# Last product of a long convolution in two column halves of TensorE, with the token rows of the input and the output stored even first, then odd

## The chip, the cores and the metric

The kernel runs on one core of a Trainium2 chip. The metric is the time of one execution on the device, in microseconds (us). Three runs of the kernel before gave 245.14, 244.03 and 245.14 us; their median is 245.14 us. The profile shows one more execution of the same program, with its own time.

The core has four compute engines that work beside each other: TensorE (PE in the profile, PEld for its weight loads), VectorE (DVE), ScalarE (ACT) and GpSimd (POOL). SyncE (SP) issues nearly all DMA transfers; a transfer, once issued, is carried out by some or all of 16 DMA engines.

## The reference

Two kinds of layer alternate, twice each, on x of 2048 tokens by 512 channels (bfloat16). Layer A is a gated long convolution, layer B an MLP of hidden width 1376. All weights are the same in both rounds.

```
def _A_ref(q, k, v, shift_k, ssm_k, ssm_D):
    ...
    k_shift = 4-tap causal convolution of k along the tokens, per channel
    kv = k_shift * v
    ...
    y = causal convolution of kv with ssm_k over 2048 tokens, by FFT
    y = y + kv * ssm_D[None, None, :]
    return q * y

def _B_ref(x, w1, b1, w2, b2):
    y = _layernorm(x, axis=-1)
    h = _gelu(jnp.einsum("bsd,df->bsf", y, w1) + b1)
    return jnp.einsum("bsf,fd->bsd", h, w2) + b2

x = A_q
x = x + _A_ref(_layernorm(x), A_k, A_v, A_shift_k, A_ssm_k, A_ssm_D)
x = x + _B_ref(_layernorm(x), B_w1, B_b1, B_w2, B_b2)
x = x + _A_ref(_layernorm(x), A_k, A_v, A_shift_k, A_ssm_k, A_ssm_D)
x = x + _B_ref(_layernorm(x), B_w1, B_b1, B_w2, B_b2)
```

(The shift and the convolution are given here in words.) Since k, v and the filters are the same in both rounds, the convolution result y is the same too, and the kernel computes it once.

## The kernel before

The kernel has two stages, and a pool of PSUM buffers for each.

**The convolution stage** (up to line 712) computes y by a transform of 2048 points that is split into factors of 32 and 64. Each factor is a matrix product with a table on TensorE; between the factors the data is turned by transposes, some on TensorE and some by DMA. Every step is a named piece, and the global order of all pieces, with the engine that runs each, is written out by hand in the string `ORDER`: `X32.P23` means that piece X32 runs on TensorE (P) and takes slot 2 of one ring of buffers and slot 3 of another; D, A, G and S are VectorE, ScalarE, GpSimd and the DMA queue of SyncE. Each engine executes its pieces strictly in that order, so a piece that has to wait holds everything that stands behind it on its engine. The pieces that matter here are:

- `lx0` (line 434) loads the first quarter of x, 4 tokens a partition, into `lna0` for the first LayerNorm. `lx` and `ly` (lines 499, 500) load x again into `x_t`, the first quarter and the other three. All three read the input `A_q` as `"(p nt) d -> p nt d"`: partition p holds the 16 tokens 16p to 16p+15, so one partition's share is one contiguous piece of memory. They are issued by SyncE through the helper `load` (line 280).
- `lk0`, `lk1`, `lv0`, `lv1` load k and v (line 280 too); `kT0` to `kT3` (line 423) transpose k on TensorE, `kT2` and `kT3` from `lk1`.
- `s00` (line 438) takes the LayerNorm statistics of `lna0` on VectorE.
- `U3T0` and `U3T1` (line 283) are DMA transposes of the first factor's result for the last quarter of the channels. `X30` and `X31` (line 515) read what U3T0 leaves, `X32` and `X33` what U3T1 leaves. In TensorE's order X32 comes before X31, and V10, X30 and the rest behind them.
- `Z01`, `Z00`, `Z20`, `Z21`, `Z03`, `Z23`, `Z10` and five more (line 584) are DMA transposes of the inverse transform's intermediate, in this order on the DMA queue behind lx; the first digit is the quarter of the channels, the second the group of tokens.
- `Y00`, `Y01`, `Y02`, `Y32`, `Y10`, `Y30`, `Y12`, `Y22`, `Y20` (line 610, in `last_mm`) are the last product. Each computes one or two columns of tokens: for every column the table `GPt`, 128 by 2 by 128, is multiplied with the two halves `V2[g][:, 0]` and `V2[g][:, 1]`, and the two products are added in PSUM. Of each 128-column half of the table, half of the columns are zero: half 0 of the table contributes to tokens of partitions with even p only, half 1 to those with odd p. Y00 needs Z00, Z10 and Z20.
- `g00` (line 635) multiplies the convolution result with the normalized x and adds it to x.

The helper `load` and its like issue a DMA whose access pattern on each side is a list of (step, count) pairs. The outermost pair comes first.

**The MLP loop** (lines 716 to 807) goes 8 times over groups of 512 tokens: `mm1` (line 726, evacuated by ScalarE with the GELU, line 728) and `mm2` (line 760, added to x by VectorE, line 765). In its second half each finished part of x is stored to the output by a DMA (line 767), 128 KB at a time, and at the very end twice 64 KB.

## Time and profile before

| | value |
|---|---|
| median of three runs | 245.14 us |
| time of the profiled execution | 245.1 us |
| its span in the profile | 243.1 us |
| convolution stage, until the MLP loop starts | 0 to 96.9 us |
| MLP loop | 96.9 to 239.5 us |
| last store, until the end | 239.5 to 243.1 us |

The span is the time between the first and the last instruction that the profiler recorded; the device time of the same execution is 2.0 us longer. In the profile, L610 is line 610 of the kernel, and "busy" of an engine counts its arithmetic alone. A row of the timeline merges successive instructions of one kind: start, length, engine, line, operation, count. SPq is SyncE's queue of DMA issues; its rows show how long the issue took, not the transfer. "us to landing" is the time from the start of an issue to the completion of the transfer.

### The profile page before, as it was taken

How to read it: one execution, taken by the hardware profiler on the slowest of the kernel's cores; microseconds unless marked ns; L12 is line 12 of the kernel's file. 1: busy time of each engine (PE TensorE's matmuls, PEld its weight loads, DVE VectorE, ACT ScalarE, POOL GpSimd, SP SyncE). 2: the span in 40 equal slices, each digit the busy share in tenths (PEclk: the TensorE clock that was granted, in tenths of full speed). 3: DMA queues.
4: the chain of work that ended last, by engine and by line, in shares of the span. 5: the costliest groups of instructions: out<-in, count | busy, mean ns of one | idle time of the engine just before them, and what ended most of it. 6: DMA issues, size and time to landing. Idle time of an engine off the chain costs nothing.

```text
span 243.1 us, 4771 instructions
## 1 busy us (share of the span) xinstructions
PE 230.3 (95%) x1941; PEld 138.5 (57%) x1941; DVE 168.2 (69%) x319; ACT 136.9 (56%) x193; POOL 38.4 (16%) x55
## 2 busy tenths in 40 slices
PE   6687999999997999999999999999999999999994
PEld 2675579889995598444444444444444444444443
DVE  0486988999998999698798977668757951031022
ACT  2563999899999998327117207307406505604700
POOL 5008694000000411301111011101101010000000
PEclk9999999999999999999999999999999999999999
DMA  8989979969899990403304030030033025011011
GB/s 133 193 235 392 380 270 379 386 146 270 197 163 171 317 250 12 86 0 25 65 0 88 0 71 18 0 74 13 4 91 83 0 62 113 0 43 43 3 43 43
DMA packets 56165, 29.55 MB, mean 122 GB/s; under 512 B 48618, under 2 KB 52431, under 8 KB 55248
## 3 DMA queue, kind: packets, MB, share of 16 engines
q1 hardware_dynamic: 56136, 29.25, 46.6%
q8 instruction: 15, 0.25, 0.4%
q14 instruction: 6, 0.05, 0.1%
q10 hardware_dynamic: 8, 0.00, 0.0%
HBM read 15.10 MB, written 2.10 MB: 71 GB/s over the span
## 4 chain that ended last, share of the span: by engine, by line
PE 80%; ACT 8%; SPq 6%; DMA 3%; issue 2%; DVE 0%; ACTq 0%
PE po L760 31%; PE ph L726 27%; PE p L670 4%; ACT ZT L212 4%; DMA Wt<-tabW 3%; SPq L280 3%; PE p L304 3%; SPq L343 3%; ACT arena L212 3%; PE p L610 3%; PE p L332 2%; PE p L538 2%; PE p L515 2%; ACT xb L212 2%; PE p L481 1%
## 5 line engine op out<-in xcount | busy, mean ns | idle before, releaser
L728 ACT ACTIVATE arena<-ph,B 128x512 bf16<-128x512 f32 (+1 forms) x77 | 52.9, 687 | 78.3 <-PE ph L726 78.2
L760 PE MATMUL po<-arena 128*128 128x512 bf16 (+2 forms) x363 | 77.4, 372 | 0.0
L726 PE MATMUL ph<-arena 128*128 128x512 bf16 (+1 forms) x308 | 67.6, 379 | 0.0
L760 PEld LDWEIGHTS <-arena 128*128 128x128 bf16 (+1 forms) x363 | 35.4, 98 | 40.5
L765 DVE TENSOR_TENSOR arena<-po,arena 128x512 bf16<-128x512 f32 (+1 forms) x33 | 21.6, 672 | 45.8 <-PE po L760 45.8
L726 PEld LDWEIGHTS <-arena 128*128 128x128 bf16 (+1 forms) x308 | 30.8, 100 | 35.9
L212 ACT ACTIVATE arena<-p 128x1024 bf16<-128x1024 f32 (+5 forms) x41 | 37.2, 1003 | 11.6 <-PE p L380 7.1
L250 POOL TENSOR_TENSOR lrsm<-lrsm,mhalf 128x4 f32<-128x4 f32 (+2 forms) x11 | 10.0, 911 | 96.9 <-DVE lrsm L244 96.9
L212 ACT ACTIVATE ZT<-p 128x1024 bf16<-128x1024 f32 (+1 forms) x26 | 24.7, 1050 | 0.9 <-PE p L304 0.8
L234 DVE BATCH_NORM_STATS2 lstm<-arena 128x6 f32<-128x512 bf16 x32 | 20.0, 681 | 0.2
L214 DVE CAST arena<-p 128x1024 bf16<-128x1024 f32 (+2 forms) x15 | 12.6, 905 | 11.0 <-PE p L374 9.7
L234 DVE BATCH_NORM_STATS2 lstg<-arena 128x6 f32<-128x512 bf16 x32 | 19.7, 678 | 0.0
L530 DVE TENSOR_TENSOR arena<-xb,arena 128x2048 bf16<-128x2048 bf16 (+1 forms) x17 | 18.9, 1153 | 0.8 <-ACT xb L212 0.7
L538 PE MATMUL p<-arena,arena 128*128 128x128 bf16 x256 | 16.1, 219 | 0.7 <-DVE arena L530 0.4
L538 PEld LDWEIGHTS <-arena 128*128 128x128 bf16 x256 | 14.8, 98 | 1.4 <-DVE arena L530 0.9
L250 POOL TENSOR_TENSOR lrsg<-lrsg,mhalf 128x4 f32<-128x4 f32 x8 | 8.1, 1012 | 41.5 <-DVE lrsg L247 41.5
L214 DVE COPY arena<-p 128x2048 bf16<-128x2048 bf16 (+2 forms) x12 | 13.3, 1109 | 1.8 <-PE p L423 1.6
L255 DVE TENSOR_SCALAR arena<-arena,lmvg,lrsg 128x512 bf16<-128x512 bf16 x28 | 9.7, 409 | 6.8 <-POOL lrsg L250 6.8
L212 ACT ACTIVATE xb<-p 128x1024 bf16<-128x1024 f32 x14 | 14.3, 1088 | 0.0
L255 DVE TENSOR_SCALAR arena<-arena,lmvm,lrsm 128x512 bf16<-128x512 bf16 x32 | 11.6, 416 | 2.4 <-POOL lrsm L250 2.4
L491 DVE TENSOR_TENSOR arena<-p,arena 128x1024 bf16<-128x1024 f32 x8 | 9.8, 1224 | 1.7 <-PE p L482 1.7
L678 ACT ACTIVATE arena<-p,B 128x128 bf16<-128x128 f32 (+3 forms) x33 | 10.0, 486 | 1.1 <-PE p L670 1.1
(70 smaller groups left out, 213.7 us busy)
## 6 DMA issues: line engine op xcount, KB each, us to landing
arena<-arena SPq DMA_DIRECT2D x8, 512.0 KB, 5.8
arena<-in_A_k_dram SPq DMA_DIRECT2D x2, 1024.0 KB, 9.7
arena<-in_A_v_dram SPq DMA_DIRECT2D x2, 1024.0 KB, 13.3
arena<-tabM SPq DMA_DIRECT2D x1, 2048.0 KB
out_dram<-arena SPq DMA_DIRECT2D x15, 128.0 KB, 1.7
arena<-in_A_ssm_k_dram SPq DMA_DIRECT2D x3, 512.0 KB, 5.6
arena<-in_A_q_dram SPq DMA_DIRECT2D x1, 1536.0 KB, 7.5
arena<-in_B_w_dram SPq DMA_DIRECT2D x1, 1376.0 KB, 6.4
```

The lines of the kernel that those rows point to most:

```text
L212: nc.scalar.activation(dst, src, AF.Copy)
L214: nc.vector.tensor_copy(dst, src)
L234: nc.vector.bn_stats(self.st[:, i, 0, :], x_t[:, GT * g + i, :] if src is None else src[:, i, :])
L250: nc.gpsimd.tensor_tensor(self.rs[:, a:b], self.rs[:, a:b], mhalf[:, a:b], ALU.pow)
L255: eng.tensor_scalar(out=dst[:, i, :], in0=xs, scalar1=self.mv[:, i, 0:1], scalar2=self.rs[:, i:i + 1], op0=ALU.subtract, op1=ALU.mult)
L530: eng.tensor_tensor(kk, x2, kk, ALU.mult)
L538: nc.tensor.matmul(o[:, i, :], spec[:, cc, ka + i, :], Mt[:, ka + i, r, :], start=r == 0, stop=r == 1)
L678: nc.scalar.activation(hT[0:m, ft, a * P:b * P], o[0:m, ft - f0, :], AF.Gelu_apprx_tanh, bias=B1[0:m, ft:ft + 1])
L726: nc.tensor.matmul(o.rearrange("p (i t) -> p i t", t=P), W1t[:, ct, ft * P:ft * P + m], lt[:, a:b, ct, :], start=ct == 0, stop=ct == CT - 1)
L728: nc.scalar.activation(hT[0:m, ft, a * P:b * P], o, AF.Gelu_apprx_tanh, bias=B1[0:m, ft:ft + 1])
L760: nc.tensor.matmul(po[:, a:b], hT[0:m, ft, i * P:(i + 1) * P], W2t[0:m, ft, a:b], start=ft == 0, stop=ft == FT - 1)
L765: nc.vector.tensor_tensor(xs, po[:, a:b], xs, ALU.add)
```

## The change

The table of the last product is cut to the columns that are not zero: half x keeps the columns of the partitions with p mod 2 = x, so `GPt` is 128 by 2 by 64. The two products of a column are no longer added in PSUM; each writes its own 64 partitions of the PSUM buffer, the even partitions' tokens to 0 to 63 and the odd ones' to 64 to 127. The result's rows therefore come out in another order: partition j holds the 16 tokens of the former partition 2j, partition 64 + j those of 2j + 1. For x to be added to it, x is loaded in the same order of rows, and the output is stored from that order back to its place. k and v, and all that is computed up to the last product, keep their order.

```
--- before.py
+++ after.py
@@ _make_tables
     GP = G[32 * (p % 4) + p // 4]
+    GP = np.stack([GP[:, x, x::2] for x in range(2)], 1)
...
-    GPt = const.tile([P, 2, P], BF16, name="GPt")
+    GPt = const.tile([P, 2, P // 2], BF16, name="GPt")
...
-        xd = q_d.rearrange(TOK, p=P)
-        lx0 = load("lx0", lna0, xd[:, 0:GT, :], 2 ** 19)
+
+        def tokens(t, a, n):
+            return apf(t, a * D, [[NT * D, 2], [2 * NT * D, P // 2], [1, n * D]])
+        lx0 = load("lx0", lna0, tokens(A_q, 0, GT), 2 ** 19)
...
-        lx = load("lx", x_t[:, 0:GT, :], xd[:, 0:GT, :], 2 ** 19, USp)
-        ly = load("ly", x_t[:, GT:, :], xd[:, GT:, :], 3 * 2 ** 19, USp)
+        lx = load("lx", x_t[:, 0:GT, :], tokens(A_q, 0, GT), 2 ** 19, USp)
+        ly = load("ly", x_t[:, GT:, :], tokens(A_q, GT, NT - GT), 3 * 2 ** 19, USp)
...
-                        nc.tensor.matmul(o[:, i, :], GPt[:, x, :], V2[g][:, x, t0 + i, :], start=x == 0, stop=x == 1)
+                        nc.tensor.matmul(o[64 * x:64 * x + 64, i, :], GPt[:, x, :], V2[g][:, x, t0 + i, :], start=True, stop=True)
...
-                    nc.sync.dma_start(out_d.rearrange(TOK, p=P)[:, GT * g + i, a:b], xs)
+                    nc.sync.dma_start(apf(out, (GT * g + i) * D + a, [[NT * D, 2], [2 * NT * D, P // 2], [1, b - a]]), xs)
```

The three loads of x and the 17 stores now have a memory side that is counted as 2 by 64 rows, where it was 128 rows; the SBUF side is still the 128 partitions. The order string is the same, and no instruction changes its place on any engine.

On SyncE, the stretch of the queue from the load of the transform table `Wt` to the last copies ahead of the table `tabM` (arena_65 and arena_66 are the places of k and v, arena_67 that of lna0) reads before:

```order
L280 DMA Wt<-tabW 128x4096
L280 DMA arena_67<-in_A_q_dram 128x2048
L280 DMA arena_65<-in_A_k_dram 128x4096
L280 DMA arena_66<-in_A_v_dram 128x4096 x2
L280 DMA GPt<-tabGP 128x256
L280 DMA arena_64<-arena_64 64x4x1024 x8
```

and now:

```order
L281 DMA Wt<-tabW 128x4096
L281 DMA arena_67<-in_A_q_dram 128x1x2048
L281 DMA arena_65<-in_A_k_dram 128x4096
L281 DMA arena_66<-in_A_v_dram 128x4096 x2
L281 DMA GPt<-tabGP 128x128
L281 DMA arena_64<-arena_64 64x4x1024 x8
```

The rows show the destination's shape: lx0 has got a third dimension to match its source of 2 by 64 rows, and the table's load is half as wide. Nothing else moved; lx0 still stands ahead of lk1, lv0 and lv1.

On TensorE, around Y00 (IDt is the identity for the transposes), before:

```order
L406 MATMUL p_125<-IDt 128x512
L610 LDWEIGHTS GPt
L610 MATMUL p_126<-arena_64,GPt 128x512
L610 LDWEIGHTS GPt
L610 MATMUL p_126<-arena_64,GPt 128x512
L572 LDWEIGHTS ZT_99
```

and now:

```order
L407 MATMUL p_125<-IDt 128x512
L613 LDWEIGHTS GPt
L613 MATMUL p_126<-arena_64,GPt 64x512
L613 LDWEIGHTS GPt
L613 MATMUL p_126<-arena_64,GPt 64x512
L575 LDWEIGHTS ZT_99
```

The number of products and of weight loads is the same; each product now writes 64 partitions instead of 128.

## The prediction

> **What bounds the kernel now.** I read the share of each engine on the path that ends last, then the stages, then the stretch that the change touches.

> ```profile
> PE 80%; ACT 8%; SPq 6%; DMA 3%; issue 2%; DVE 0%; ACTq 0%
> 77.20:84.50 7.30, 7.03 (x53) 3.89 (x52) 6.99 (x21) 7.30 (x11) 2.37 (x3) 1.00 1.05 284
> 84.50:90.20 5.70, 5.70 (x102) 5.62 (x101) 5.19 (x15) 5.70 (x18) 0.82 (x2) 1.00 1.09 229
> 90.20:96.70 6.50, 6.50 (x55) 5.12 (x54) 6.36 (x16) 5.53 (x15) 1.07 (x1) 1.00 0.19 65
> 96.90:239.50 142.60, 142.60 (x671) 66.05 (x669) 87.06 (x203) 55.54 (x84) 13.31 (x14) 1.00 0.19 40
> ```

> TensorE makes 80% of the chain. In the rows by stage (busy time of PE, PEld, DVE, ACT and POOL, then clock, DMA share and GB/s) it is busy all of the 142.6 us of the MLP loop, which the change leaves alone. The last product lies at 77.2 to 92 us, and there ScalarE is busy without a gap too (7.30 of 7.30, 5.70 of 5.70). So time can be won in some 15 us, and lost wherever TensorE is made to wait.

> **The products.**

> ```profile
> 79.48 3.67 PE L610 MATMUL p<-arena,GPt 128*128 128x512 bf16 x16 [0.28 <-ACT arena L212]
> 90.19 1.89 PE L610 MATMUL p<-arena,GPt 128*128 128x512 bf16 x8
> 15.83 2.39 PE L380 MATMUL p<-Ft,arena 128*64 128x128 bf16 x64
> 59.94 0.61 PE L515 MATMUL p<-arena,Wt 128*128 128x128 bf16 x8
> ```

> 16 products take 3.67 us, about 0.22 each, so all 32 take 7 us. Products into 64 partitions exist already, at L380: 64 of them with 128 columns take 2.39 us, 0.037 each, where full ones of that width (L515, x8 in 0.61) take 0.055 once the run-out of the last is taken off. Two halves thus run partly beside each other. With 512 columns, a pair should take between one product's 0.22 and 0.63 of two, 0.28, where it takes 0.44 now: at most 3.5 us of TensorE are freed. Until 90.2 us, ScalarE's evacuations set the pace and nothing comes of it; the last group (8 products in 1.89 us) has only TensorE ahead of it and gets 0.8 us shorter. Bounds: 0 and -3.5; I take **-0.8 us**. The smaller table's load is hidden: it stands on the queue ahead of the convolution's copies, and its first use is Y00 at 77.29 (row below).

> **What the loads and stores become.** The memory side of five kinds of transfer gets a leading count of 2. How are the rows of such a transfer dealt out? Two transfers of this program have a small leading count already: the one on ScalarE's queue (line 183, 4 rows of 1 KB) and the taps' load (line 351, source 4 by 32 rows of 128 bytes, destination 128 partitions, the same form as the new loads).

> ```profile
> q10 hardware_dynamic: 8, 0.00, 0.0%
> DMA packets 144, 0.07 MB, mean 101 GB/s; under 512 B 16, under 2 KB 144, under 8 KB 144
> DMA packets 47, 0.12 MB, mean 396 GB/s; under 512 B 33, under 2 KB 33, under 8 KB 33
> DMA packets 45, 0.10 MB, mean 330 GB/s; under 512 B 33, under 2 KB 33, under 8 KB 33
> ```

> The second row is a 64 KB store of today (239.55 to 240.2 us): 144 packets are 128 rows and 16 small ones, one from each engine at its end. The first transfer leaves 8: 4 rows and 4 small ones, so four engines. The last two rows are 18.18 to 18.48 us and 18.49 to 18.80 us, in the taps' load: each holds 33 packets under 512 bytes, 32 rows and a small one, in 0.3 us, one row every 9.4 ns. That is a quarter of the 128 rows, one after the other, as one engine would do them; sixteen engines would have 8 each and be done in a quarter of that time. Both transfers use as many engines as their leading count. I conclude that the changed ones run on **two engines of 16**.

> [...] By a rule that spread the 128 partitions whatever the source's form, the sum below would be only its first term.

> What does one engine move? From 25.5 to 29 us the loads of k and v keep all busy:

> ```profile
> DMA packets 198, 1.48 MB, mean 424 GB/s; under 512 B 17, under 2 KB 17, under 8 KB 17
> q1 hardware_dynamic: 198, 1.48, 100.2%
> ```

> 424 GB/s over 16 engines is 26.5 GB/s each. lx0 and lx (0.52 MB) take 1.2 us on 16 engines and 9.9 on two, 8.7 more; ly (1.57 MB) 3.7 and 29.7 us, 26.0 more. What is queued behind them on those two engines lands as much later.

> **lx0.**

> ```profile
> arena<-in_A_q_dram SPq DMA_DIRECT2D x1, 512.0 KB, 8.5
> 15.94 0.61 SPq L280 DMA_DIRECT2D arena<-in_A_k_dram  x1
> arena<-in_A_k_dram SPq DMA_DIRECT2D x1, 1024.0 KB, 10.5
> 27.20 1.16 PE L423 MATMUL p<-IDt,arena 128*128 128x128 bf16 x16
> 26.09 2.46 DVE L234 BATCH_NORM_STATS2 lstg<-arena 128x6 f32<-128x512 bf16 x4
> arena<-in_A_v_dram SPq DMA_DIRECT2D x2, 1024.0 KB, 13.3
> 31.94 2.44 DVE L491 TENSOR_TENSOR arena<-p,arena 128x1024 bf16<-128x1024 f32 x2 [0.41 <-PE p L482]
> ```

> lx0 is issued at 15.47 (the row ahead of lk1's on the queue) and lands at 24.0 us; lk1, behind it, is issued at 15.94 and lands at 26.4. TensorE needs lk1 for kT3 at 27.20, VectorE needs lx0 for s00 at 26.09. With 8.7 us more, lx0 lands at 32.7 and lk1 at 35.1: s00 waits 6.6, kT3 up to 7.9 us, and everything stands behind kT3. lv0 and lv1, issued from 16.6 us on, land 13.3 later, at about 30, and now at 39, which is when VectorE, itself 7 us late, first needs them (31.94 now): no more is lost. If the two engines are among those that start lx0 early, it is some 2 us less. Bounds 5.5 and 8; I take **+7 us**.

> **ly and lx.**

> ```profile
> 51.50 1.10 SPq L280 DMA_DIRECT2D arena<-in_A_q_dram  x1
> arena<-in_A_q_dram SPq DMA_DIRECT2D x1, 1536.0 KB, 7.5
> 52.66 6.16 SPq L283 DMA_TRANSPOSE arena<-ZT  x1
> arena<-ZT SPq DMA_TRANSPOSE x1, 9.6
> 64.92 1.15 PE L515 MATMUL p<-arena,Wt 128*128 128x128 bf16 x16
> 58.88 0.57 SPq L280 DMA_DIRECT2D arena<-in_A_q_dram  x1
> arena<-in_A_q_dram SPq DMA_DIRECT2D x1, 512.0 KB, 4.6
> 66.36 2.61 SPq L584 DMA_TRANSPOSE arena<-ZT  x2
> 77.29 0.59 PE L610 MATMUL p<-arena,GPt 128*128 128x512 bf16 x2
> 78.89 0.69 DVE L639 TENSOR_TENSOR arena<-arena,p 128x512 bf16<-128x512 bf16 x1
> ```

> ly lands at 59.0, the transpose U3T1 behind it at 62.3, and its issue holds the queue for 6.16 us: it goes through behind ly. X32 uses it at 64.92. With ly 26.0 us later (all times here before the 7 us), U3T1 lands at 88.3 and X32, with all of TensorE's order behind it, waits 23.4 us. Next on the two engines is lx, issued at 58.88 and landed at 63.5 now: with both delays, 63.5 + 26.0 + 8.7 = 98.2. Behind it stand Z01, Z00, Z20, Z21, Z03, Z23 and Z10, whose issues take 1.3 us each (2.61 for two). With 9.1 us for the seven and about 1 until the last has landed, Z10 is there at 108. By then TensorE has come to Y00 (77.29 + 23.4 = 100.7) and waits for it: Y00 starts 30.7 us later than now. Bounds: X32's wait alone, 23.4, if the Z transposes are not held; 35, if each takes the 1.8 of the slowest of its kind. Y00's wait could be 2 us shorter again for engines that start early; I take **+30 us**. lx is then in time for g00 (78.89 now, behind Y00), and so is w1, two transposes behind Z10, whose first user stands behind most of the Y pieces.

> **The stores.**

> ```profile
> 234.82 5.50 SPq L767 DMA_DIRECT2D out_dram<-arena  x5
> 239.54 0.42 DVE L765 TENSOR_TENSOR arena<-po,arena 128x256 bf16<-128x256 f32 x1 [0.78 <-PE po L760]
> q1 hardware_dynamic: 144, 0.13, 55.6%
> q1 hardware_dynamic: 144, 0.07, 34.5%
> out_dram<-arena SPq DMA_DIRECT2D x2, 64.0 KB, 1.5
> 13.82 0.76 SPq L280 DMA_DIRECT2D arena<-in_A_shift_k_dram  x1
> ```

> The third and fourth row are one 128 KB store (0.7 us from 219.6) and one 64 KB store (0.65 us from 239.55): 0.131 MB in 0.7 x 16 x 55.6% = 6.2 engine-us, 21 GB/s an engine; 0.066 MB in 3.6, 18 GB/s. On two engines that is 3.1 and 1.8 us. The last group's three large and two small stores need 12.9 us from the first's start at about 235.6, until 248.5. The last one's issue now ends at 240.3 and takes 0.3, and it lands 1.5 after its start, at 241.5. Bounds: +7.5 with half a us for the landing, +5.5 if each row takes a tenth less; I take **+6.5 us**. Earlier stores end well ahead of these. They hold the loop's transposes a few us, which are needed 20 us after their issue: nothing. The longer issue of such a transfer (the taps' took 0.76 us, lx 0.57) is hidden behind the backlog.

> **The clock.** The profile grants 1.00 everywhere, yet TensorE begins slowly:

> ```profile
> 2.00:4.00 2.00, 1.96 (x5) 0.73 (x6) 0.00 (x0) 1.41 (x2) 0.55 (x3) 1.00 1.16 185
> 5.00:6.00 1.00, 1.00 (x5) 0.44 (x4) 0.00 (x0) 0.00 (x0) 0.54 (x2) 1.00 1.34 215
> ```

> The same five products take 1.96 and then 1.00 us; one us is lost there, and in the us and a half around it perhaps 0.7 more. The new pauses of 7, 23 and some 6 us may each cost that again, or nothing. The second restart is covered by Y00's wait, the third partly by ScalarE. Bounds 0 and +3.4; I take **+1 us**. [...]

> **Sum**, against the profiled execution's 245.1 us (the median is the same): 245.1 - 0.8 + 7 + 30 + 6.5 + 1 = 288.8, **289 us**.

> **Rivals.**
> - *All 16 engines after all* (not slower): the destination's 128 partitions decide. Then only the products' gain is left, less up to 0.4 us for the longer issue of the last store: 245.1 - 0.8 + 0.2 = 244.5. For it: the SBUF side still leads with 128. Against: so does the taps' load. It decides by the count of engines: already on 8, ly takes 3.7 us more and U3T1 lands at 66.0, 1.1 after X32's time, more than the 0.8 won. Chance 0.03.
> - *Two engines, but what stands behind is not held* (transposes are served between the rows of ly). Then only direct users wait: s00 6.6 us, and g00 for lx, which shares the two engines with ly until 52.6 (the end of ly's issue) + 29.7 + 9.9 = 92.2, or 98.8 with the first delay; g00 stands at 78.89 today, so 20 us in all: 245.1 + 20 + 6.5 - 0.8 = 271. For it: nothing but the separate kind of transfer. Against: U3T1's landing right behind ly. Chance 0.1.
> - *Two engines that are slower alone*, by memory latency between rows: at half the rate lx0 and lx take 9.9 us longer still, ly 29.7, the stores 12.9: 289 + 9.9 + 39.6 + 12.9 = 351. Against: the taps' rows followed each other without gaps. Chance 0.04.

> **How the numbers follow.** My case has 0.83. Its terms' bounds give 245.1 + 5.5 + 23.4 + 5.5 - 3.5 = 276 and 245.1 + 8 + 35 + 7.5 + 3.4 = 299. With the rivals' 0.17 left out and a little for the ends, that is 8 in 10: **276 to 299**. Only the first rival is within 0.5% (about what a measurement of this kernel can tell from no change) or below: faster 0.01, same 0.02, slower 0.97.

> **What would show it.** The last products' pairs at 0.22 to 0.28 us; lx0, ly and lx landing some 9, 33 and 42 us later; TensorE idle before kT3, X32 and Y00; a DMA share near 2 of 16 in those waits; the last stores ending 6 to 7 us later. The prediction is wrong if stores or loads of x keep their landing times, or if U3T1 lands while ly still moves.

## The result, and the profile after

| | before | after |
|---|---|---|
| median | 244.99 us (six runs) | 299.91 us (six runs) |
| lowest to highest | 244.03 to 245.16 us | 298.62 to 300.39 us |
| profiled execution, its span | 245.1, 243.1 us | 300.39, 298.3 us |

The ratio is 1.2227 (95% interval 1.2181 to 1.2273). One run of the changed kernel, of 1339.74 us, counts in its median alone (299.72 us without it); and where a kernel's runs spread, as E1's below, the ratio goes by the least disturbed ones and lies under that of the medians.

The change costs 55 us. The prediction was 289.0 with a range of 276 to 299: the sign and the two engines came out; the size, and what TensorE waits for, did not. First the page of the changed kernel (tenths in 40 slices of 7.5 us, then the chain of work that ended last) and what TensorE waited for (us in total, times, longest):

```profile
PE   6877199999100039889999999999999999999960
PEclk9995769999955558999999999999999999999995
DMA  8999238991111934998030402120301706201011
PE 63%; issue 13%; DMA 8%; DVE 5%; SPq 5%; ACT 2%; POOL 0%; ACTq 0%
PE p L541 <- issue: 34.0, 1, 34.0
PE p L424 <- DMA arena<-in_A_k_dram: 7.4, 2, 7.1
PE p L391 <- DMA Wt<-tabW: 3.0, 1, 3.0
```

TensorE's share of the chain fell from 80% to 63%. It stops twice (slices counted from 1): in slices 5 and 6, where the wait for `lk1` (7.1 us) has a DMA share of 2 to 3 tenths, and in slices 11 to 15; in 11 to 13 the share is 1 tenth, about two engines of 16. The second wait has a name that the prediction did not have: not a DMA, but "issue", a time in which TensorE waits for nothing that the profile shows. TensorE's timeline (start, length, line, operation, count, idle time before):

```profile
37.69 1.93 PE p L424 x16
74.75 0.89 PE L541 MATMUL p<-arena,arena 128*128 128x128 bf16 x13
109.63 3.91 PE L541 MATMUL p<-arena,arena 128*128 128x128 bf16 x35 [33.99 <-issue]
126.26 0.41 PE L613 MATMUL p<-arena,GPt 128*64 128x512 bf16 x2
139.24 1.05 PE L613 MATMUL p<-arena,GPt 128*64 128x512 bf16 x8
145.40 9.68 PE L763 MATMUL po<-arena 128*128 128x512 bf16 x43
```

(The first row, from the chain, is kT3.) V22 is the block of 48 products that comes just ahead of X32. It begins at 74.75 us, where it began at 62.24:

```profile
62.24 2.84 PE L538 MATMUL p<-arena,arena 128*128 128x128 bf16 x48
```

That row of the kernel before has all 48 in one piece; now 13 run, TensorE stands for 34 us, and 35 follow. Set against the kernel before, stage by stage:

| stretch | before | after | difference | predicted |
|---|---|---|---|---|
| start to V22 | 62.24 | 74.75 | +12.5 | +7, and +1 for all restarts |
| V22 to Y00 | 15.05 | 51.51 | +36.5 | +30 |
| Y00 to the MLP loop | 19.43 | 19.14 | -0.3 | -0.8 |
| loop start to VectorE's last addition | 142.8 | 142.8 | 0 | 0 |
| last addition to the end | 3.56 | 10.08 | +6.5 | +6.5 |

The sum, 55.2, is the difference of the spans.

### The profile page after: what moved, and what is told of

Its sections match the earlier page's. It is cut to its first block, busy times and chain, and to the rows that moved or that the text cites. A ratio compares the mean times of both kernels' runs of the same rounds, so it can differ in the third digit from the quotient of the medians.

```text
span 298.3 us, 4760 instructions
## 1 busy us (share of the span) xinstructions
PE 234.8 (79%) x1930; PEld 142.0 (48%) x1941; DVE 168.7 (57%) x319; ACT 137.7 (46%) x193; POOL 38.4 (13%) x55
## 4 chain that ended last, share of the span: by engine, by line
PE 63%; issue 13%; DMA 8%; DVE 5%; SPq 5%; ACT 2%; POOL 0%; ACTq 0%
PE po L763 25%; PE ph L729 22%; DMA arena<-in_A_k_dram 7%; PE p L541 3%; SPq L281 3%; PE p L305 2%; SPq L344 2%; PE p L518 2%; PE p L333 2%; PE p L673 2%; PE p L424 1%; PE p L484 1%; PE p L391 1%; DMA arena<-arena 1%; PE p L485 1%
## 5 line engine op out<-in xcount | busy, mean ns | idle before, releaser
L763 PE MATMUL po<-arena 128*128 128x512 bf16 (+3 forms) x355 | 77.0, 372 | 0.4
L213 ACT ACTIVATE arena<-p 128x1024 bf16<-128x1024 f32 (+5 forms) x41 | 37.6, 1000 | 23.6 <-PE p L391 8.9
L541 PE MATMUL p<-arena,arena 128*128 128x128 bf16 x256 | 17.9, 232 | 34.9 <-issue 34.0
L541 PEld LDWEIGHTS <-arena 128*128 128x128 bf16 x256 | 16.5, 105 | 35.5 <-issue 34.6
L215 DVE CAST ZT<-p 128x1024 bf16<-128x1024 f32 x3 | 3.7, 1219 | 34.4 <-PE p L541 34.4
L215 DVE COPY arena<-p 128x2048 bf16<-128x2048 bf16 (+2 forms) x12 | 13.3, 1112 | 4.2 <-PE p L424 4.1
L391 PE MATMUL p<-arena,Wt 128*128 128x512 bf16 x29 | 11.0, 517 | 3.4 <-DMA Wt<-tabW 3.0
L256 DVE TENSOR_SCALAR arena<-arena,lmvm,lrsm 128x512 bf16<-128x512 bf16 x32 | 11.5, 416 | 2.4 <-POOL lrsm L251 2.4
## 6 DMA issues: line engine op xcount, KB each, us to landing
arena<-arena SPq DMA_DIRECT2D x8, 512.0 KB
arena<-in_A_k_dram SPq DMA_DIRECT2D x2, 1024.0 KB
arena<-in_A_v_dram SPq DMA_DIRECT2D x2, 1024.0 KB
arena<-in_A_ssm_k_dram SPq DMA_DIRECT2D x3, 512.0 KB
arena<-in_A_q_dram SPq DMA_DIRECT2D x1, 1536.0 KB
```

What stands on the lines that cost most here:

```text
L213: nc.scalar.activation(dst, src, AF.Copy)
L215: nc.vector.tensor_copy(dst, src)
L256: eng.tensor_scalar(out=dst[:, i, :], in0=xs, scalar1=self.mv[:, i, 0:1], scalar2=self.rs[:, i:i + 1], op0=ALU.subtract, op1=ALU.mult)
L391: nc.tensor.matmul(o[:, i, :], Wt[:, 2 * j + i, :], Zk[:, 2 * j + i, :], start=True, stop=True)
L541: nc.tensor.matmul(o[:, i, :], spec[:, cc, ka + i, :], Mt[:, ka + i, r, :], start=r == 0, stop=r == 1)
L763: nc.tensor.matmul(po[:, a:b], hT[0:m, ft, i * P:(i + 1) * P], W2t[0:m, ft, a:b], start=ft == 0, stop=ft == FT - 1)
```

## The experiments

Each edit is against the kernel named. "Halves" means that a transfer is issued as two, for 64 partitions each, so that no access pattern begins with a count of 2.

**E1, all x transfers in halves** (against the changed kernel):

```
+ for x in range(2):
+     nc.sync.dma_start(dst[64 * x:64 * x + 64], apf(A_q, (x * NT + a) * D, [[2 * NT * D, P // 2], [1, n * D]]))
```

> The changed kernel with each of the three loads of x and each store issued as two transfers of 64 partitions, the even rows and the odd rows, so that the leading count is 64 and not 2; the last product stays in two column halves. Theory (all of the loss comes from two DMA engines doing the work of 16): the loss is gone, 244 to 246 us, within 1% of the kernel before; what is left of the product's gain is 0 to 1 us, against 17 more store issues. Rival (the half products or the new order of rows themselves cost): well above 250 us. Rival (a stall in TensorE's code supply that has nothing to do with these transfers): TensorE still stops for tens of us in the middle of the products of line 541.

Measured: 251.01 us (247.18 to 252.46) beside 244.95, ratio 1.0107 (1.0038 to 1.0176). With the leading count of 2 gone, about nine tenths of the 55 us are gone; it was the cause. But by the ratio 2.6 us stay, by the medians 6, which I did not expect. E8 and E11 look for them. In E1's profiled execution, 6.5 us longer than the one before, 4.1 lie ahead of V22, 1.1 behind the last addition, and 1.6 in V22, which stops after the same 13th product as in the changed kernel (E1's timeline):

```profile
68.82 2.13 PE L547 MATMUL p<-arena,arena 128*128 128x128 bf16 x35 [1.56 <-issue]
```

So a stop of this kind, a short one, comes without the leading count of 2 too.

**E2, E1 with ly alone as one transfer with the leading count of 2:**

```
- ly = halves("ly", x_t[:, GT:, :], GT, NT - GT, 3 * 2 ** 19, USp)
+ ly = load("ly", x_t[:, GT:, :], tokens(A_q, GT, NT - GT), 3 * 2 ** 19, USp)
```

> As e1_halves, but ly (1.5 MB) is one transfer with leading count 2 again. Theory A (TensorE's own instructions come over the same DMA engines, and their fetch waits until the long run of ly's rows on its engine is over): TensorE stops in the middle of V22 at about 63 us, with nothing that it waits for in the profile, and the queue-8 transfer of 16 KB that falls at about 59 us before starts only when ly's last row is through, at about 84. Theory B (as predicted: U3T1 is queued behind ly): TensorE runs on through V22, V23 and V21 and waits at X32 from about 65 to 87 us. Both give about 267 to 273 us in all; the place of the stop tells them apart.

Measured: 277.38 us, above the range that I expected. The stop in V22 is there, as in the changed kernel (E2's timeline):

```profile
92.91 3.88 PE L547 MATMUL p<-arena,arena 128*128 128x128 bf16 x35 [25.94 <-issue]
```

**E3, E2 with ly as twelve transfers of one token a partition**, each still with the leading count of 2, so as many bytes on as many engines, but in shorter runs:

```
+ for i in range(GT, NT, 1):
+     nc.sync.dma_start(x_t[:, i:i + 1, :], tokens(A_q, i, 1))
```

> As e2_ly, but ly is issued as 12 transfers of one token a partition, each with leading count 2: the same bytes on the same two engines, in 12 runs of 64 rows of 1 KB instead of one run of 64 rows of 12 KB. Theory A (the fetch gets its turn only between two transfers' runs on an engine): the fetch gets in after 3 to 6 us, TensorE does not stop in V22 and waits at X32 instead, for U3T1, which lands when ly is through, at about 88 us; 267 to 273 us in all. If the fetch waits until the whole queue of the engine is empty, whatever its runs, TensorE stops in V22 as in e2_ly.

Measured: 277.13 us, above what I expected too, but the place moved as Theory A had it. V22 runs through, and the wait stands where the prediction put it, at X32 (E3's timeline):

```profile
94.66 1.89 PE L528 MATMUL p<-arena,Wt 128*128 128x128 bf16 x16 [24.64 <-DMA arena<-ZT]
```

What stopped V22 in E2 is seen in the DMA rows. One queue, q8, carries 15 transfers of 16 KB called "instruction". TensorE is the only engine with that many (1930 products and 1941 weight loads recorded, some 258 for each), so I read them as its next instructions. In the kernel before, the sixth comes at 58.95 us; the row of 58 to 60 us (packets, MB, share of 16 engines):

```profile
q8 instruction: 1, 0.02, 3.5%
```

In E3 it comes at 61.7 us, with ly under way:

```profile
q8 instruction: 1, 0.02, 3.8%
```

In the changed kernel there is none from 62.5 to 97 us (all that these 34.5 us hold, first fence), but one at 97.9 (97.5 to 99.5 us, second fence):

```profile
q1 hardware_dynamic: 3251, 2.36, 119.6%
q14 instruction: 1, 0.01, 0.1%
```

```profile
q8 instruction: 1, 0.02, 3.4%
```

In E2 it comes at 90.2 us, when ly's rows (57.2 to 88.6) are through, and V22 goes on 1.6 us after it has landed. In E1, E4, E5, E7, E10, E11 and E12 V22 stops after the same product and goes on 1.4 to 1.7 us after this transfer has landed. So what it lacks is its instructions.

What holds the instructions is less clear. By an estimate, ly's rows alone can: in E1, where ly is on all 16 engines, the fifth transfer comes at 53.0 us. In E3 the sixth follows the fifth after 7.9 us, so in E1 it was due at 60.9, ahead of U3T1's rows (from 64.4). It comes at 66.2, when ly's rows (57.5 to 65.4) are through. In E2 and the changed kernel there is a second candidate, the transpose U3T1 behind ly. In the changed kernel SyncE needs 31.55 us to issue it, 18 of its rows begin at 66.6 to 67.0 us and end 30 us later (most of the 119.6% above), and the instructions come when U3T1's last row is nearly through as well. E3 took away both candidates: SyncE needs 28.10 us to issue the twelve transfers and comes to U3T1 only then (SyncE's timeline, the changed kernel's U3T1 in the first fence, E3's ly and U3T1 in the second):

```profile
64.96 31.55 SPq L284 DMA_TRANSPOSE arena<-ZT  x1
```

```profile
56.45 28.10 SPq L512 DMA_DIRECT2D arena<-in_A_q_dram  x12
84.60 7.85 SPq L284 DMA_TRANSPOSE arena<-ZT  x1
```

So with twelve transfers of short rows the instructions get through and the data is late instead; whether ly's long rows or the transpose's waiting ones hold them in E2 is not shown.

**E4, E1 with lx0 alone with the leading count of 2:**

```
- lx0 = halves("lx0", lna0, 0, GT, 2 ** 19)
+ lx0 = load("lx0", lna0, tokens(A_q, 0, GT), 2 ** 19)
```

> As e1_halves, but lx0 (0.5 MB) is one transfer with leading count 2 again. From the changed kernel's trace: lx0's 64 rows on each of two engines take 14.5 us beside the loads of k and v (10 was predicted from the rate of full loads), lk1 lands at 37.6 instead of 26.4, kT3 is 10.5 us late, and the clock granted to TensorE falls to one half twice, which adds 2 us: 257 to 258 us in all. If the 10 us of the prediction were right and the rest came from the other transfers: 252 to 253.

Measured: 260.34 us, 9.3 more than E1; the wait for `lk1` is 8.9 us. More than expected, and more than the prediction's 7.

**E5, E1 with the stores alone with the leading count of 2:**

```
- for x in range(2):
-     nc.sync.dma_start(apf(out, (x * NT + GT * g + i) * D + a, [[2 * NT * D, P // 2], [1, b - a]]), xs[64 * x:64 * x + 64])
+ nc.sync.dma_start(apf(out, (GT * g + i) * D + a, [[NT * D, 2], [2 * NT * D, P // 2], [1, b - a]]), xs)
```

> As e1_halves, but the 17 stores have leading count 2 again. Theory: 64 rows of 1 KB at 46 ns on each of two engines, 3 us a store, make a backlog in the last group; the last store lands some 6 us later than in the kernel before, against which e1_halves itself has lost about 1 us there: 255 to 257 us. Rival (stores to memory are not bound by the engine): 250 to 252, as e1_halves.

Measured: 254.84 us, just under the range that I expected. From the last addition's start (242.92) to the span's end (252.8) it takes 9.9 us, as in the changed kernel. In E1 it takes 4.65, so 5.2 of it are the leading count's. The time rose by less, 3.8, since E5's last addition came 2.0 us earlier than E1's: in its start TensorE waited 2.6 us for `Wt`, in E1's 3.6, and its stop in V22 was 1.1 us, not 1.6.

**E6, the changed kernel with only ly cut into twelve**, as in E3:

> The changed kernel itself (lx0, lx and all stores with leading count 2), but ly as 12 transfers of one token a partition, each with leading count 2. ly's bytes, engines and place on the queue are the same. If the fetch of TensorE's instructions behind ly's and lx's single long runs is what the prediction missed after X32's time: TensorE reaches X32 and waits there for U3T1, until some 100 us instead of stopping in V22 until 109.6; then Y00 waits for Z10 behind lx and starts at about 119 instead of 126: 291 to 294 us in all, 6 to 9 less than the changed kernel's 300. If the stop in V22 only takes the place of the waits that come anyway: 299 to 301.

Measured: 297.02 us, ratio 1.2063 (1.1974 to 1.2152), about 3 us less than the changed kernel; I had expected 6 to 9. Here the waits are those of the prediction, X32 and then Y00 (E6's timeline):

```profile
75.17 2.84 PE L551 MATMUL p<-arena,arena 128*128 128x128 bf16 x48
102.42 1.89 PE L528 MATMUL p<-arena,Wt 128*128 128x128 bf16 x16 [24.41 <-DMA arena<-ZT]
122.87 0.64 PE L623 MATMUL p<-arena,GPt 128*64 128x512 bf16 x2 [7.33 <-DMA arena<-ZT]
```

It had 23.4 us for X32 and 7.3 for Y00. But as in E3, U3T1 is late because SyncE comes to it late, at 92.49 us, after 27.98 us of issuing ly. So E6 has the size of the wait at X32, but not a transpose held on the two engines; that is U3T1 in the changed kernel. Y00 begins 47.7 us after V22, 32.7 more than before.

**E7, E1 with lx alone with the leading count of 2:**

```
- lx = halves("lx", x_t[:, 0:GT, :], 0, GT, 2 ** 19, USp)
+ lx = load("lx", x_t[:, 0:GT, :], tokens(A_q, 0, GT), 2 ** 19, USp)
```

> As e1_halves, but lx (0.5 MB) has leading count 2 again. Theory A (instruction fetch held by a long run): the fetch that falls at 63 to 66 us meets lx's run of 10 us and TensorE stops for 5 to 10 us in V22: 256 to 261 us. If only the Z transposes behind lx are held: no stop in V22, Y00 is late by 0 to 5 us: 251 to 256.

Measured: 261.83 us, 10.8 more than E1, in another place than I expected: V22's stop is 1.3 us, no longer than E1's, and X32 waits for U3T1 (E7's timeline):

```profile
79.62 1.89 PE L524 MATMUL p<-arena,Wt 128*128 128x128 bf16 x16 [8.37 <-DMA arena<-ZT]
```

U3T1 was issued ahead of lx, at 57.96 us, and landed when lx's run (69.3 to 79.2) was over. So such a run also held what was issued shortly before it. In E6 U3T1 landed ahead of lx; why the two differ stays open.

The four parts alone add 26.4, 9.3, 10.8 and 3.8 to E1's 251.0, together 301.3: they add up to the changed kernel's 299.9 within 1.4 us. That it fits so closely is in part luck: each of the four is a single run, and E1's own runs spread over 5.3 us.

**E12, the changed kernel with lx alone in halves.** In the changed kernel the instructions come at 97.9 us, but TensorE stays idle until 109.6. Is that lx?

```
- lx = load("lx", x_t[:, 0:GT, :], tokens(A_q, 0, GT), 2 ** 19, USp)
+ lx = halves("lx", x_t[:, 0:GT, :], 0, GT, 2 ** 19, USp)
```

> The changed kernel with lx alone as two transfers of 64 partitions; lx0, ly and the stores keep their leading count of 2. Theory A (TensorE's missing instructions come when ly's run ends, near 97 us, and what kept it idle until 109.6 us in the changed kernel is lx's run of 64 rows on the same two engines): TensorE stops in V22 at about the same place, for some 23 to 25 us instead of 34, resumes 1 to 3 us after ly's end and does not wait for Z's; time about 10 us less than the changed kernel, 288 to 292 us. Rival B (the end of the stop is set by something other than lx, such as the transposes that stand behind ly, or the end of the instruction transfer itself): the stop stays at 32 to 35 us and the time at 298 to 301.

Measured: 290.36 us (290.05 to 291.48), ratio 1.1822 (1.1735 to 1.191). The stop is 24.8 us and ends 1.7 us after the instructions have landed (E12's timeline):

```profile
101.18 3.92 PE L547 MATMUL p<-arena,arena 128*128 128x128 bf16 x35 [24.82 <-issue]
```

So some 9 of the 34 us are lx's. Which of TensorE's needs lx's rows held after the instruction transfer had landed is not shown.

**E10, E1 with each half of ly as 62 and 2 partitions.** A leading count of 2 put ly on two engines (12.5% of the 16, 78 to 95 us of the changed kernel), counts of 64 on all (99.8% in E11, 57 to 60 us). Only 2 and 1 of the numbers up to 16 divide 62; are 62 rows dealt to two engines, or to sixteen?

```
+ for j, w in ((0, 62), (62, 2)):
+     nc.sync.dma_start(x_t[64 * x + j:64 * x + j + w, GT:, :], apf(A_q, ((x + 2 * j) * NT + GT) * D, [[2 * NT * D, w], [1, (NT - GT) * D]]))
```

> As e1_halves, but each half of ly (64 partitions) is issued as one transfer of 62 partitions and one of 2; no transfer has a leading count of 2 and a second one behind it. If the number of engines is the largest up to 16 that divides the count of rows, 62 = 2 x 31 gives two engines: ly takes 30 us again, as in e2_ly, 270 to 278 us in all; the instruction fetch gets in after a run of 31 rows (14 us), so TensorE's stop is in V22 for up to 14 us and then at X32. If a transfer of 62 rows is dealt to 16 engines: 250 to 253, as e1_halves.

Measured: 280.73 us, a little above the range of the two-engine case and far from the other's. The stop in V22 is back, 29.6 us. So it isn't the form of 2 by 64 that costs, but the small number of engines, which 62 rows got too: from 58 to 90 us E10 moves 50 GB/s, where the two engines of the changed kernel move 53 (78 to 95 us). One expectation failed: the instructions did not get in between two runs. The first 64 partitions are through at 75.7 to 77.4 us on the two engines, but the instructions come at 93.8, when ly (to 92.1) is through and U3T1 nearly. Shorter runs alone did not let them in here.

**E8, E1 with the odd halves issued by ScalarE:**

```
- for x in range(2):
-     nc.sync.dma_start(dst[64 * x:64 * x + 64], ...
+ for x, q in enumerate((nc.sync, nc.scalar)):
+     q.dma_start(dst[64 * x:64 * x + 64], ...
```

> As e1_halves, but of each of the three loads of x the even half is issued by SyncE and the odd half by ScalarE, so that both halves are under way at once on every engine. e1_halves' rows of 12 KB took 939 ns (median of the packets), twice the 460 of the kernel before. [...] If the rows are slow because a half has rows of twice the step in memory: 939 as before, 249 to 252.

Measured: 248.55 us (247.14 to 249.44), ratio 1.0115 (1.0048 to 1.0181), as E1's. The two halves did not run beside each other: ly's even half moved from 55.9 to 60.3 us, its odd half from 64.6 to 68.4. So the run does not tell whether two halves at once would be as fast as one whole transfer.

**E11, the kernel before, old row order and old products, with its x loads and stores as two transfers of 64 neighbouring partitions:**

```
+ for x in range(2):
+     nc.sync.dma_start(dst[64 * x:64 * x + 64], xd[64 * x:64 * x + 64, a:a + n, :])
```

> The kernel before, in its own order of rows and with its own products, with each load of x and each store issued as two transfers of 64 neighbouring partitions. In e1_halves and e8_two_queues the rows of 12 KB of a half took 925 to 939 ns each, against 460. e8_two_queues did not tell why, because the halves did not overlap. If 64 partitions at a time are what halves the rate: 900 to 950 here too, stores' rows about 70 ns instead of 46, and the time 247 to 252 us, as e1_halves. If the doubled step in memory is: 460 and 46 ns, and 244 to 247 us.

Measured: 250.12 us. With the old order of rows this single run keeps about as much of the loss as E1, so what E1 keeps comes from moving 64 partitions at a time, not from the new order. Three us of ly, in the kernel before (54 to 57 us) and in E11 (57 to 60 us):

```profile
DMA packets 85, 1.04 MB, mean 348 GB/s; under 512 B 0, under 2 KB 0, under 8 KB 0
q1 hardware_dynamic: 85, 1.04, 92.7%
```

```profile
DMA packets 62, 0.65 MB, mean 217 GB/s; under 512 B 9, under 2 KB 9, under 8 KB 9
q1 hardware_dynamic: 62, 0.65, 99.8%
```

All engines are busy in both. 85 rows of 12 KB took 44.5 engine-us (busy time summed over the engines), 0.52 each; in E11 53 rows took 47.9, 0.90 each.

**E9, the kernel before with the new products alone**; loads and stores keep the old order, so the convolution's rows are added to other rows of x:

```
+ GP = np.stack([GP[:, x, x::2] for x in range(2)], 1)
- nc.tensor.matmul(o[:, i, :], GPt[:, x, :], V2[g][:, x, t0 + i, :], start=x == 0, stop=x == 1)
+ nc.tensor.matmul(o[64 * x:64 * x + 64, i, :], GPt[:, x, :], V2[g][:, x, t0 + i, :], start=True, stop=True)
```

> The kernel before with the last product in two column halves and the table cut, and nothing else: loads, stores and their order of rows stay as before, so the result's rows are added to the wrong rows of x. It times the product alone. In the changed kernel's trace 8 half products take 1.05 us against 1.89 and the stretch from Y00 to the MLP loop 19.1 us against 19.4. If ScalarE's evacuations hide the rest: 0.3 us less than before, a ratio of 0.998 to 1.000. The prediction's term was 0.8 us less. If TensorE's 3.5 freed us counted: 241 to 242 us.

Measured: 244.66 us beside 245.01, ratio 0.9974 (0.9948 to 1.0001). The span of its profiled execution is 242.8, 0.3 less than before: as much as the stretch from Y00 to the loop became shorter in the changed kernel, but no more than the comparison can tell from nothing.

No version beats the kernel before: the halved product is worth 0.3 us if anything, and of the two ways tried to bring x in its order of rows the cheaper costs 3 to 6.

## Why the prediction was right, and where it was wrong

**What the transfers become: right.** Two engines (E1 against the changed kernel; E10 takes the same count from another form). While ly moves alone, 78 to 95 us of the changed kernel:

```profile
DMA packets 74, 0.91 MB, mean 53 GB/s; under 512 B 0, under 2 KB 0, under 8 KB 0
q1 hardware_dynamic: 74, 0.91, 12.5%
```

That is 2 of 16 engines with 26.5 GB/s each, the prediction's rate; ly took 30.5 us (65.8 to 96.3), the prediction had 29.7. The rivals of sixteen engines and of two engines at half rate fall by this; that of "not held" falls by U3T1 in the changed kernel, whose issue behind ly takes 31.55 us, where it took 6.16.

**lx0, "+7" with bounds of 5.5 and 8: mis-sized.** kT3 began 10.5 us later (27.20 to 37.69). The step that failed is "424 GB/s over 16 engines is 26.5 GB/s each" for a transfer that moves beside the loads of k and v: lx0's 128 rows took 14.6 us, not 9.9, 18 GB/s an engine. Of the same rows of 4 KB, lx0's took 0.22 us each in the median and lx's, later and almost by themselves, 0.16. The two engines did not get less than the others. From 23 to 29 us of the changed kernel all 16 are busy, and together they move only 264 GB/s, 16.5 each, where they moved 424 in the prediction's row:

```profile
DMA packets 239, 1.58 MB, mean 264 GB/s; under 512 B 23, under 2 KB 23, under 8 KB 69
q1 hardware_dynamic: 239, 1.58, 100.9%
```

The rows of 8 KB of k and v are slower as well in this stretch, 0.50 us in the median, where they took 0.31 before. Why a mixture of the two kinds of transfer slows all engines is open. s00 shows the same delay (35.2 us, predicted 32.7):

```profile
35.21 2.47 DVE L235 BATCH_NORM_STATS2 lstg<-arena 128x6 f32<-128x512 bf16 x4 [6.56 <-DMA arena<-in_A_q_dram]
```

E4, with lx0 alone, agrees: +9.3.

**The clock, "+1" with bounds of 0 and 3.4: at the upper bound and above.** Stretches of the changed kernel (busy time of PE, PEld, DVE, ACT and POOL, then the granted clock, DMA share and GB/s):

```profile
22.80:29.40 6.60, 5.38 (x13) 2.02 (x15) 2.45 (x2) 3.16 (x4) 3.44 (x3) 0.50 1.00 266
33.20:43.00 9.80, 5.09 (x36) 4.21 (x38) 4.69 (x10) 1.02 (x1) 4.69 (x6) 0.50 0.12 50
109.60:112.60 3.00, 2.97 (x29) 2.98 (x30) 0.66 (x1) 1.02 (x1) 0.00 (x0) 0.50 0.43 91
```

The first piece begins within the 3.0 us wait for `Wt` (1.1 before), the second within the wait for `lk1`, the third is the end of the one that began in the long stop. The first costs nothing here, since `lk1` is later still. The second costs 2.0 us: from kT3 to V22 it takes 37.06 us, where it took 35.04. The third costs 2.3: from the end of the stop to Y00 it takes 16.6 us, from the same place in V22 14.3 before. Together 4.3, worked out from the trace; no run changes the clock alone. The 1 that I took from the start of the kernel was too little. When the clock falls is not the same everywhere: the first row is of a piece that began during a wait of only 3.0 us, in a stretch with other gaps, and in the long stops the clock fell 2.1 us (E10), 5.0 us (the changed kernel) and 5.2 us (E3) after the last product, so the runs show no fixed time.

**ly and lx, "+30" with bounds of 23.4 and 35: right in what becomes late, wrong in what TensorE waits for.** Worked out were 23.4 us at X32 and 7.3 at Y00; E6 has 24.4 and 7.3 there, though U3T1 is late in another way. The step that failed is the one that let TensorE come to X32 at all: "what is queued behind them on those two engines lands as much later" was applied to data alone. TensorE's instructions come over DMA engines too, by my reading of q8, and were held as long (25.9 us of stop in E2), and it ran out of them inside V22, about 2 us ahead of X32. Its stop of 34.0 us replaces the two waits of 31.7. With the slower restart's 2.3 this is nearly the 36.5. Against E6, where the instructions come in time, it costs 3 us. By the spans the change costs 55.2 us, and the prediction's terms make 43.7. Of the 11.5 that it lacked, lx0 has 3.5, the clock 3.3, this term 4.2 (36.5 less 2.3, against 30), and the products 0.5; no single one is most of the miss.

**The stores, "+6.5": right.** 3.56 to 10.08 us, +6.5; the last group's rows took 11.9 us (284.7 to 296.5), a little less than the 12.9 worked out from the kernel before.

**The products, "-0.8": mis-sized.** The last eight products take 1.05 us, where they took 1.89, so the step from widths of 128 to pairs at 0.28 was too careful: from two products in 0.41 to eight in 1.05 a further pair adds 0.21, and the halves run fully beside each other. But only 0.3 us of the 0.84 arrive (E9, where they are not clear of noise). The next work on TensorE, in the kernel before and in the changed one:

```profile
91.92 4.97 PE L670 MATMUL p<-arena 128*128 128x256 bf16 x44
```

```profile
140.60 4.96 PE L673 MATMUL p<-arena 128*128 128x256 bf16 x44 [0.30 <-ACT arena L681]
```

It came 1.73 us after the first of the eight products (90.19) and comes 1.36 after it now (139.24), of which it waits 0.30 for ScalarE, which it did not before. The prediction had "only TensorE ahead of it"; ScalarE is close behind.

## What to carry to other kernels

Look at the outermost count of every DMA whose access pattern is changed: 2 on the memory side with 128 partitions on the other (the changed kernel), or 62 rows (E10), put it on two engines here, at 53 and 50 GB/s. Then price not only who reads its data but all that stands behind it on those engines, the instructions of a busy engine among them. A wait called "issue" in the middle of a loop of equal instructions, at a time when a few DMA engines have long runs, pointed to missing instructions here (E2: the stop of 25.9 us ended 1.6 us after the next instruction transfer had landed): look when that transfer lands. Twelve transfers of short rows, with the transpose issued behind them, let the instructions through here (E3, E6); the same long rows in four transfers did not (E10). And a saving on TensorE that stands in one stage of 15 us should be weighed against the way in which all other data must be laid out for it.
